# Attention and MoE in one kernel: a new order for norms, turns and sums in the first attention

## The chip, the cores and the metric

The kernel runs on one core of a Trainium2 chip. The metric is the device time of one execution in microseconds; the median of several runs is taken. Engines: PE (matmul), ACT (ScalarE), DVE (VectorE), POOL (GpSimd), SP (DMA queues).

## What is computed

Attention with normed q and k over 8 batches, 12 heads, 448 positions, head width 64, and then a two-layer network with a gelu between (768 to 2048 to 768) on all 3,584 tokens:

```
q_n, k_n = rmsnorm(q, g_q), rmsnorm(k, g_k)          # over the 64 of a head
attn = softmax(q_n @ k_n.T / 8)                      # (8, 12, 448, 448)
x = (attn @ v) -> (3584, 768)                        # heads side by side
out = gelu_tanh(x @ w_in) @ w_out                    # 768 -> 2048 -> 768
```

## The kernel before

The work goes batch by batch. Within a batch the 12 heads are taken in NCH = 3 groups `c` of four heads, and the 448 positions as 7 blocks `t` of 64. A *unit* is one pair (c, t): four small matmuls (64 by 64 weights, 448 columns) that make scores, keys on the partitions and queries along the columns, in one of two PSUM score tiles that alternate. In the first attention unit number i is (i // 7, i % 7), so i runs from 0 to 20. Units 2 to 13 get a constant added by four more matmuls ahead of the scores (L342). ACT turns a unit's scores into exponentials (`exp`, L355), in a buffer `ex` for all seven blocks of a group; there are two such buffers, so that group 2 (units 14 to 20) writes the one that group 0 had.

`products(b, c, what, lo, hi)` multiplies the exponentials of blocks lo to hi - 1 on PE (L400): with `what` 0 by ones, which gives the sums of the softmax (here *sums*), with 1 by v (here *V products*). Each block is a *group* of four small matmuls, two into each of two PSUM tiles. The sums are turned by DVE (`turned`, L411), inverted (`recip`, L416), spread again (`spread`, L423), and multiplied with the V products into `xT` (`quad_x`, L441), the input of the first layer. `mm1_pair` and `mm1` (L565, L450) are the first layer: PE matmuls of 128 by 128 weights over pieces of `xT`; pieces 2c and 2c + 1 come of group c.

Ahead of a unit's scores, q and k have to be squared (`square`), summed over the head (`total`, L174, DVE), taken to the power -1/2 (`rsqrt`, ACT: a logarithm L199, then exponentials L215, L218 into PSUM for DVE and L206 into SBUF for GpSimd), multiplied (`normed`, L277, on DVE or POOL), turned by PE (`turn`, L295) into a PSUM tile, and copied to SBUF by DVE (`put`, L304 for k, L308 for q). `t_first` is blocks 0 to 3 and `t_rest` blocks 4 to 6, so that k can go in two pieces. The roots for DVE stand in PSUM: those of group 1 in spare columns of the second of the two tiles `oall` that the products of the first attention write (`place`), those of the last group in a tile of their own from the pool `ps_m`, which has two buffers and also gives the tiles for the turns and for sums (`spared`).

The order of instructions on every engine is written out by hand: `first_attention` emits, for every i, the unit, its exponential, and then the entries of the list `mid` with that number. What an entry does is queued on its engine behind what earlier entries gave it; waits between engines follow from the tiles that are read and written. After unit 20 the function emits the last sums and V products and the first pieces of the first layer. GpSimd's list holds the norms of group 2's q, squares of the next batch, and the issue of the transfers of w_in, w_out and v.

Of the kernel before, what the change touches and what calls it, by code (L numbers as in the profile page):

```python
# [17 lines left out]
def kernel(  # L18
# [11 lines left out]
    nc = tc.nc  # L30
# [147 lines left out]


    oall = [ps_o.tile([128, 512], F32, tag=f"o{r}", name=f"o{r}") for r in range(2)]  # L180
    roots, places = {}, {}

    def place(b, c):
        if (b, c) == (0, NCH - 1):
            t = ps_m.tile([128, 512], F32, tag="mm", name="root")[:, :4 * NT]
        else:
            i = c % 2 * 4 * NT
            t = oall[1][:, S + i:S + i + 4 * NT]
        roots["qk", b, c] = t.rearrange("p (n a t) -> p n a t", n=2, a=2)
        for n in range(2):  # L190
            roots.setdefault(("qk"[n], b, c), roots["qk", b, c][:, n])
        return t

    def rsqrt(b, c=slice(0, NCH), ns=both, near=(), ts=slice(0, NT), twice=False):

        if b not in rinvs:
            rinvs[b] = smp.tile([P, NCH, 2, 2, NT], F32, tag="rinv", name="rinv")
# [12 lines left out]
        if near:  # L210
# [5 lines left out]
            else:  # L216
                t = roots["qk"[near[0]], b, c]
                nc.scalar.activation(t[:, :, ts], lg[:, c, near[0], :, ts], AF.Exp, scale=-0.5)  # L218
        to_sbuf([n for n in range(2)[ns] if n not in near])

    def rsqrt_newton(b):

# [65 lines left out]
    tps = {}  # L288

    def turn(b, c, n, ts=slice(0, NT)):  # L290

# [136 lines left out]
    def recips():  # L428
        recip()
        spread()  # L430
# [144 lines left out]
        )  # L575

    early, late = range(HP - 2), range(HP - 2, HP)
    even, odd = early[::2], early[1::2]

    STEADY = (  # L580
# [135 lines left out]
    def first_attention(side, mid):  # L716

        for i in range(NCH * NT):
            for fn in side.get(i, ()):
                fn()  # L720
            unit(0, i // NT, i % NT)
            exp(0, i // NT, i % NT)
            for fn in mid.get(i, ()):
                fn()
        nc.scalar.preload_act_table_set(GELU_SET)
        c = NCH - 1
        products(0, c, 0, 6)
        turned()
        products(0, c, 1, 5)
        recips()  # L730
        mm1_pair(0, even)
        quad_x(0, c)
        mm1_pair(1, even)
        mm1_pair(0, odd)
        mm1_pair(1, odd)

        mm1(0, 4, early)
        mm1_pair(0, late)
        mm1_pair(1, late)
        square(1, 1, "q", nc.scalar)  # L740
        mm1(0, 4, late)
# [55 lines left out]
    def warm():  # L797
        return oall[0][:, :S]
# [67 lines left out]
    def turn_new(c, ts):  # L866
        tps["k"] = ps_m.tile([128, 1024], BF16, tag="mm", name="tp")
        turn(0, c, "k", ts)

    mid = [(0, lambda: idle(1, warm())),  # L870
           (1, lambda: square(0, 1, "k", nc.scalar, slice(1, 2)),
            lambda: total(0, 1, "k", slice(1, 2)),
# [5 lines left out]
           (4, lambda: idle(1, warm())),  # L878
           (5, lambda: turn(0, 1, "q"), lambda: put(0, 1, "q")),
           (6, lambda: turn_new(1, t_first), lambda: put(0, 1, "k", slice(0, 1)),  # L880
            lambda: put(0, 1, "k", slice(1, 4)),
            lambda: total(0, 2, "q"), lambda: total(0, 2, "k")),
           (7, lambda: products(0, 0, 0, 0, 2)),
           (8, lambda: products(0, 0, 0, 2, 5), lambda: normed(0, 1, "k", nc.vector, t_rest),
            lambda: rsqrt(0, 2, near=(1,)), lambda: normed(0, 2, "q", nc.gpsimd),
            lambda: square(1, 0, "q", nc.gpsimd), lambda: w_in_part(1, 2),
            lambda: square(1, 0, "k", nc.gpsimd),
            lambda: w_out_part(0, 4), lambda: w_out_part(4, 8),
            lambda: square(1, 2, "q", nc.gpsimd), lambda: square(1, 2, "k", nc.gpsimd),
            lambda: w_out_part(8, 12), lambda: w_out_part(12, 14),  # L890
            lambda: w_out_part(14, 16), lambda: load_v(1, 0, 2), lambda: load_v(1, 2, 4),
            lambda: normed(0, 2, "k", nc.vector, t_first)),
# [165 lines left out]
```

## Time and profile before

| | |
|---|---|
| median of 3 runs | 393.44 us (393.36 to 393.51) |
| the profiled execution | 394.93 us |
| its span, first to last instruction | 392.9 us |
| granted PE clock | 0.999 |
| PE, ACT, DVE, POOL busy in the span | 384.7, 277.7, 237.2, 124.3 us |

The profile is of one execution. The span lacks about 2 us around it. In a row of a timeline stand the start, the length, the engine, the line of the kernel, the operation, what it writes and reads with shapes, the number of instructions merged, and in brackets the idle time of the engine before it with what ended it. Starts are counted from the span's start.

### The profile page before, as it was taken

The page shows a single profiled execution, that of the slowest core. Times are in us where ns is not written, and L with a number is a line of the kernel's source. Part 1 is how long each engine was busy: PE and PEld are TensorE (multiplying, and loading weights), DVE is VectorE, ACT ScalarE, POOL GpSimd, SP SyncE. Part 2 cuts the span into 40 slices and gives each one's busy share as a digit, 9 for nine tenths or more (in the row PEclk, how much of TensorE's full clock was granted, in tenths as well). Part 3 has the DMA queues.
Part 4 walks back from the last instruction along what each step waited for, and adds up shares of the span by engine and source line. Part 5 has one row for each costly group of instructions (what it writes and reads, how often), then busy time and mean ns, then how long its engine had stood idle before and what let it go on. Part 6 is the DMA issues. An engine that isn't in the chain of part 4 may idle for free.

```text
span 392.9 us, 17557 instructions
## 1 busy us (share of the span) xinstructions
PE 384.7 (98%) x8066; PEld 291.8 (74%) x8066; DVE 237.2 (60%) x369; ACT 277.7 (71%) x354; POOL 124.3 (32%) x106
## 2 busy tenths in 40 slices
PE   8899999989999999999999999999999999999996
PEld 3455567868868788877888778887888778887664
DVE  5888947975589257953589265963599304880010
ACT  6984589757996589946997579946897449944300
POOL 5995504484102740074301840054400900000000
PEclk9999999999999999999999999999999999999999
DMA  8999998999722995269932896159722621120033
GB/s 280 314 230 211 210 153 274 239 199 245 131 65 63 217 220 102 48 110 247 199 82 55 173 261 116 44 100 208 150 60 75 114 53 41 44 64 4 2 81 81
DMA packets 64414, 54.68 MB, mean 139 GB/s; under 512 B 37588, under 2 KB 59988, under 8 KB 64340
## 3 DMA queue, kind: packets, MB, share of 16 engines
q1 hardware_dynamic: 53904, 41.33, 43.9%
q0 software_dynamic: 10128, 11.80, 18.3%
q8 instruction: 63, 1.03, 1.1%
q10 hardware_dynamic: 308, 0.43, 0.3%
q14 instruction: 11, 0.09, 0.1%
HBM read 45.61 MB, written 11.01 MB: 144 GB/s over the span
## 4 chain that ended last, share of the span: by engine, by line
PE 91%; DVE 3%; ACT 3%; issue 1%; DMA 1%; DVEq 0%
PE t L546 32%; PE t L504 30%; PE t L400 9%; PE t L347 7%; PE t L477 5%; PE t L565 4%; ACT ex L355 2%; PE tp L295 1%; PE o L400 1%; DMA rawq<-in_q_dram 1%; PE h L450 1%; DVE ss L174 0%; DVE kT L304 0%; ACT L1014 0%; PE t L342 0%
## 5 line engine op out<-in xcount | busy, mean ns | idle before, releaser
L504 PE MATMUL t<-wout,g 64*64 64x384 bf16 (+1 forms) x3456 | 150.8, 305 | 0.0
L355 ACT ACTIVATE ex<-t,shift 128x896 bf16<-128x896 f32 x156 | 145.2, 1016 | 3.4 <-PE t L347 1.9
L546 PE MATMUL t<-xT,win 64*64 64x448 bf16 x2688 | 128.9, 349 | 1.1 <-issue 1.1
L504 PEld LDWEIGHTS <-g 64*64 64x64 bf16 x3456 | 112.7, 107 | 20.0 <-PE t L504 0.3
L546 PEld LDWEIGHTS <-win 64*64 64x64 bf16 x2688 | 98.0, 107 | 30.6 <-issue 1.5
L552 ACT ACTIVATE g<-t 128x896 bf16<-128x896 f32 x56 | 50.5, 915 | 59.1 <-PE t L546 59.1
L174 DVE TENSOR_REDUCE ss<-sq 128x14 f32<-128x896 f32 (+3 forms) x45 | 44.5, 997 | 53.8 <-ACT sq L163 50.1
L347 PE MATMUL t<-qT,kT 64*64 64x448 bf16 x672 | 58.3, 350 | 0.7 <-DVE shifts L853 0.3
L368 DVE TENSOR_TENSOR es<-ex 128x1792 bf16<-128x1792 bf16 x20 | 21.2, 1058 | 33.2 <-ACT ex L355 33.2
L277 POOL TENSOR_TENSOR nrmq<-rawq,rinv 128x896 bf16<-128x896 f32 (+1 forms) x21 | 34.8, 1657 | 20.2 <-ACT rinv L206 12.2
L802 POOL COPY mark<-es 1x1 bf16<-1x1 bf16 x6 | 1.1, 178 | 117.7 <-DVE es L375 113.6
L277 POOL TENSOR_TENSOR nrmk<-rawk,rinv 128x896 bf16<-128x896 f32 x20 | 33.6, 1680 | 0.0
L400 PE MATMUL t<-ex,vb 64*64 64x448 bf16 x588 | 31.9, 350 | 0.0
L347 PEld LDWEIGHTS <-kT 64*64 64x64 bf16 x672 | 25.4, 106 | 6.9 <-DVE kT L304 1.5
L411 DVE STREAM_TRANSPOSE st<-t 128x448 f32<-128x448 f32 x42 | 24.7, 627 | 9.1 <-PE t L400 9.1
L400 PEld LDWEIGHTS <-vb 64*64 64x64 bf16 x672 | 23.0, 107 | 7.5 <-issue 0.8
L423 DVE STREAM_TRANSPOSE rb<-rc 128x896 f32<-128x896 f32 (+1 forms) x25 | 26.7, 1067 | 0.3
L710 DVE COPY osb<-t 128x384 f32<-128x384 f32 (+1 forms) x4 | 2.0, 507 | 35.2 <-PE t L477 35.2
L436 DVE TENSOR_TENSOR xT<-t,rb 128x896 bf16<-128x896 f32 x21 | 22.8, 1085 | 0.8
L165 POOL TENSOR_TENSOR sq<-rawq 128x896 f32<-128x896 f32 (+1 forms) x9 | 13.6, 1511 | 29.3 <-DVE ss L174 29.2
L522 ACT COPY osb<-t 128x768 f32<-128x768 f32 (+1 forms) x18 | 12.6, 698 | 14.0 <-PE t L504 14.0
L371 DVE TENSOR_TENSOR es<-es,ex 128x1792 bf16<-128x1792 bf16 x20 | 21.2, 1062 | 0.7 <-ACT ex L355 0.7
(107 smaller groups left out, 327.7 us busy)
## 6 DMA issues: line engine op xcount, KB each, us to landing
rawq<-in_q_dram SPq DMA_DIRECT2D x23, 448.0 KB, 5.1
rawk<-in_k_dram SPq DMA_DIRECT2D x23, 448.0 KB, 5.8
out_dram<-osb SPq DMA_DIRECT2D x42, 192.0 KB, 2.7
vb<-in_v_dram POOLq DMA_DIRECT2D x6, 672.0 KB, 7.5
win<-in_moe_w_in_dram POOLq DMA_DIRECT2D x8, 384.0 KB, 11.6
wout<-in_moe_w_out_dram POOLq DMA_DIRECT2D x3, 768.0 KB, 18.1
out_dram<-osb SPq DMA_DIRECT2D x24, 96.0 KB, 3.4
vb<-in_v_dram POOLq DMA_DIRECT2D x2, 448.0 KB, 15.3
```

The source lines that it names most:

```text
L174: nc.vector.reduce_sum(sss[b][:, seat(b, c), "qk".index(n), hs, ts], squares(b, c, n, hs, ts), axis=AX.X)
L277: eng.tensor_mul(nrms[n, b, c][:, ts].rearrange("p t a d -> p a t d"), raws[n, b, c][:, :, ts], root[:, :, ts].to_broadcast([P, 2, m, D]),)
L347: nc.tensor.matmul(sc[r * R:(r + 1) * R, a, :S], kT[rs, c, t, r], qT[b][rs, c, :, r], start=not begun, stop=True,)
L355: nc.scalar.activation(exs[b, c][:, t], scs.pop((b, c, t))[:, :, :S], AF.Exp, scale=scale, bias=0.0 if in_psum(b, c, t) else shift)
L368: nc.vector.tensor_add(es, ex[:, :2], ex[:, 2:4])
L400: nc.tensor.matmul(o[r][a * D:(a + 1) * D], vb[b % 2][rs, 2 * c + a, i] if what else ones[rs], es[i][rs, a], start=(i == 0), stop=(i == n ...
L411: nc.vector.transpose(oas["st"][:, r].rearrange("p a b -> p (a b)"), o[r])
L423: nc.vector.transpose(oas["rb"][:, rs].rearrange("p r s -> p (r s)"), rc.to_broadcast([128, (rs.stop - rs.start) * m, 32]),)
L436: nc.vector.tensor_mul(xT[b][:, 2 * c:2 * c + 2], oas["o", c, 1][:, :, :S], oas["rb"])
L504: mm = nc.tensor.matmul(o[a * R:(a + 1) * R, bank, :hi - lo], g[rs, f, at:at + R], wout[rs, f, lo:hi], start=(turn == 0 and f == 0), stop= ...
L546: mm = nc.tensor.matmul(h[a * R:(a + 1) * R, j, :S], win[rs, c, at:at + R], xT[b][rs, c], start=begin and c == cs[0], stop=end and c == cs ...
L552: nc.scalar.activation(g[:, 2 * i:2 * i + 2, (b % 2) * S:(b % 2 + 1) * S], h[:, :, :S], AF.Gelu_apprx_tanh,)
```

## The change

- The norm of the middle group's k rest (`normed(0, 1, "k", nc.vector, t_rest)`) goes from entry 8 to entry 6, ahead of the totals of group 2.
- The roots of group 2 are made in entry 9 instead of 8, now both into SBUF too (`also`); POOL norms q of group 2 in two pieces and the rest of its k, which DVE did in entry 12. The transfers and squares behind it on POOL stay behind it; w_in's second part now goes ahead of both squares of group 0 of the next batch.
- q of group 2 is turned into the tile that holds the roots (`tps["last"]`, the same bank), in two pieces (`turn_last`), each followed by its put. Before it had a tile of its own and was turned at once.
- The turn of the middle k's rest goes from entry 10 to 9, the V products of group 0 end behind unit 15 instead of behind unit 14, and the sums and V products of group 1 shift likewise.
- All sums of group 2 stand ahead of its V products; the first two pieces of the first layer's first pair of tiles stand between them.

```diff
     def place(b, c):
         if (b, c) == (0, NCH - 1):
-            t = ps_m.tile([128, 512], F32, tag="mm", name="root")[:, :4 * NT]
+            own = ps_m.tile([128, 512], F32, tag="mm", name="root")
+            tps["last"] = own.bitcast(BF16)
+            t = own[:, S:S + 4 * NT]
...
-        to_sbuf([n for n in range(2)[ns] if n not in near])
+        to_sbuf([n for n in range(2)[ns] if also or n not in near])
...
         products(0, c, 0, 6)
         turned()
-        products(0, c, 1, 5)
         recips()
-        mm1_pair(0, even)
+        mm1_pair(0, early[:2])
+        products(0, c, 1)
         quad_x(0, c)
-        mm1_pair(1, even)
-        mm1_pair(0, odd)
-        mm1_pair(1, odd)
+        mm1_pair(0, early[2:])
+        mm1_pair(1, early)
...
+    def turn_last(ts):
+        tps["q"] = tps["last"]
+        turn(0, 2, "q", ts)
+        put(0, 2, "q", ts)
+
...
            (6, lambda: turn_new(1, t_first), lambda: put(0, 1, "k", slice(0, 1)),
-            lambda: put(0, 1, "k", slice(1, 4)),
+            lambda: put(0, 1, "k", slice(1, 4)), lambda: normed(0, 1, "k", nc.vector, t_rest),
             lambda: total(0, 2, "q"), lambda: total(0, 2, "k")),
            (7, lambda: products(0, 0, 0, 0, 2)),
-           (8, lambda: products(0, 0, 0, 2, 5), lambda: normed(0, 1, "k", nc.vector, t_rest),
-            lambda: rsqrt(0, 2, near=(1,)), lambda: normed(0, 2, "q", nc.gpsimd),
-            lambda: square(1, 0, "q", nc.gpsimd), lambda: w_in_part(1, 2),
-            lambda: square(1, 0, "k", nc.gpsimd),
+           (8, lambda: products(0, 0, 0, 2, 5)),
+           (9, lambda: products(0, 0, 0, 5), lambda: turn(0, 1, "k", t_rest),
+            lambda: put(0, 1, "k", t_rest), lambda: turned(rs=range(1)),
+            lambda: rsqrt(0, 2, near=(1,), also=True),
+            lambda: normed(0, 2, "q", nc.gpsimd, t_first),
+            lambda: normed(0, 2, "q", nc.gpsimd, t_rest),
+            lambda: normed(0, 2, "k", nc.gpsimd, t_rest), lambda: w_in_part(1, 2),
+            lambda: square(1, 0, "q", nc.gpsimd), lambda: square(1, 0, "k", nc.gpsimd),
...
-            lambda: normed(0, 2, "k", nc.vector, t_first)),
-           (9, lambda: products(0, 0, 0, 5)),
-           (10, lambda: turn(0, 1, "k", t_rest), lambda: put(0, 1, "k", t_rest),
-            lambda: turned(rs=range(1))),
-
-           (11, lambda: turn(0, 2, "k", t_first), lambda: put(0, 2, "k", t_first),
-            lambda: turned(rs=range(1, 2))),
-           (12, lambda: turn(0, 2, "q"), lambda: put(0, 2, "q"),
-            lambda: normed(0, 2, "k", nc.vector, t_rest), lambda: recip(),
+            lambda: normed(0, 2, "k", nc.vector, t_first), lambda: turned(rs=range(1, 2))),
+
+           (12, lambda: turn(0, 2, "k", t_first), lambda: put(0, 2, "k", t_first),
+            lambda: turn_last(t_first)),
+           (13, lambda: turn_last(t_rest), lambda: recip(), lambda: products(0, 0, 1, 0, 3),
             lambda: spread(slice(0, 1))),
-           (13, lambda: products(0, 0, 1, 0, 3), lambda: turn_new(2, t_rest),
-            lambda: put(0, 2, "k", t_rest), lambda: spread(slice(1, 2))),
-
-           (14, lambda: products(0, 0, 1, 3), lambda: quad_x(0, 0)),
-           (15, lambda: spared(), lambda: products(0, 1, 0, 0, 4)),
-           (16, lambda: products(0, 1, 0, 4), lambda: turned(), lambda: recips()),
-           (17, lambda: products(0, 1, 1, 0, 4)),
-           (18, lambda: products(0, 1, 1, 4), lambda: quad_x(0, 1)),
-           (19, lambda: spared(), lambda: products(0, 2, 0, 0, 3)),
-           (20, lambda: products(0, 2, 0, 3, 5), lambda: products(0, 2, 1, 0, 5),
-            lambda: products(0, 2, 0, 5, 6))]
+           (14, lambda: turn_new(2, t_rest), lambda: put(0, 2, "k", t_rest),
+            lambda: spread(slice(1, 2)), lambda: products(0, 0, 1, 3, 5)),
+           (15, lambda: products(0, 0, 1, 5), lambda: quad_x(0, 0),
+            lambda: spared(), lambda: products(0, 1, 0, 0, 2)),
+           (16, lambda: products(0, 1, 0, 2, 5)),
+           (17, lambda: products(0, 1, 0, 5), lambda: turned(), lambda: recips()),
+           (18, lambda: products(0, 1, 1, 0, 3)),
+           (19, lambda: products(0, 1, 1, 3), lambda: quad_x(0, 1)),
+           (20, lambda: spared(), lambda: products(0, 2, 0, 0, 6))]
```

More of the change, by code (lines that the diff above doesn't have):

```diff
@@ L180 @@
     oall = [ps_o.tile([128, 512], F32, tag=f"o{r}", name=f"o{r}") for r in range(2)]
-    roots, places = {}, {}
+    roots, places, tps = {}, {}, {}
     def place(b, c):
         if (b, c) == (0, NCH - 1):
-            t = ps_m.tile([128, 512], F32, tag="mm", name="root")[:, :4 * NT]
+            own = ps_m.tile([128, 512], F32, tag="mm", name="root")
+            tps["last"] = own.bitcast(BF16)
+            t = own[:, S:S + 4 * NT]
         else:
@@ L192, in place, with rsqrt @@
         return t
-    def rsqrt(b, c=slice(0, NCH), ns=both, near=(), ts=slice(0, NT), twice=False):
+    def rsqrt(b, c=slice(0, NCH), ns=both, near=(), ts=slice(0, NT), twice=False, also=False):
         if b not in rinvs:
@@ L286, in qT_of @@
         return qT[b]
-    tps = {}
     def turn(b, c, n, ts=slice(0, NT)):
@@ L577 @@
     early, late = range(HP - 2), range(HP - 2, HP)
-    even, odd = early[::2], early[1::2]
     STEADY = (
```

## The prediction

> **What bounds the kernel now.** I read the page first, for what the end is made of, then the busy time of each engine by stretches, and then the timelines of the stretch that is edited, one engine at a time.
>
> ```profile
> PE 384.7 (98%) x8066; PEld 291.8 (74%) x8066; DVE 237.2 (60%) x369; ACT 277.7 (71%) x354; POOL 124.3 (32%) x106
> PE 91%; DVE 3%; ACT 3%; issue 1%; DMA 1%; DVEq 0%
> ```
>
> The first is the busy time of the engines, the second the chain that ended last: PE carries it. The stretches:
>
> ```profile
> 15.90:24.70 8.80, 7.92 (x137) 4.19 (x133) 7.81 (x15) 6.73 (x11) 8.03 (x11) 1.00 1.14 249
> 24.70:31.10 6.40, 5.96 (x110) 3.53 (x106) 5.05 (x9) 6.38 (x7) 6.39 (x6) 1.00 1.12 219
> 31.10:36.40 5.30, 5.30 (x55) 2.85 (x44) 4.09 (x7) 1.30 (x2) 2.94 (x5) 1.00 1.13 210
> 36.40:80.20 43.80, 43.75 (x732) 29.14 (x730) 35.34 (x76) 35.06 (x44) 15.64 (x15) 1.00 1.03 218
> ```
>
> Each row gives the length, then busy time and instruction count of PE, PEld, DVE, ACT and POOL, then the granted clock, DMA share and GB/s. From 31.1 us PE has no idle time worth the name, at the full clock. So the end moves by as much as PE's arrival at its unbroken run moves, and only the first attention, up to there, can move it. Inside it no engine is the bound alone: from 15.9 to 24.7 PE is busy 7.92 of 8.80 us, DVE 7.81; from 24.7 to 31.1 ACT is busy 6.38 of 6.40. The order of waits decides. All edits lie in those two stretches, and the work of PE in them is the same before and after. The profiled span is 392.9 us; that execution lasted 394.93, against a median of 393.44, so what I work out is a difference of spans, and I add it to the median.
>
> The rows that carry the argument, from the timelines of PE, and then of ACT, DVE and POOL (one row with a bar is from the groups of that stretch by shape, with count, busy time and mean ns; the last is the page's for the w_in transfers, with size and us to landing):
>
> ```profile
> 15.93 0.55 PE L400 MATMUL o<-ex,ones 64*64 64x448 bf16 x8
> 16.31 0.36 PE L342 MATMUL t<-eighth,shifts 64*64 64x448 bf16 x4
> 16.49 0.36 PE L347 MATMUL t<-qT,kT 64*64 64x448 bf16 x4
> ...
> 17.44 0.36 PE L347 MATMUL t<-qT,kT 64*64 64x448 bf16 x4
> 17.63 0.35 PE L400 MATMUL o<-ex,ones 64*64 64x448 bf16 x2
> 18.48 0.57 PE L400 MATMUL o<-ex,ones 64*64 64x448 bf16 x6 [0.50 <-DVE nrmk L277]
> ...
> 20.21 0.38 PE L347 MATMUL t<-qT,kT 64*64 64x448 bf16 x4 [0.20 <-DVE kT L304]
> 20.53 0.40 PE L295 MATMUL tp<-ident,nrmk 128*128 128x128 bf16 x4
> ...
> 23.23 0.34 PE L295 MATMUL tp<-ident,nrmk 128*128 128x128 bf16 x3
> 23.50 0.38 PE L347 MATMUL t<-qT,kT 64*64 64x448 bf16 x4
> 23.71 0.93 PE L400 MATMUL o<-ex,vb 64*64 64x448 bf16 x16
> 24.47 0.36 PE L347 MATMUL t<-qT,kT 64*64 64x448 bf16 x4
> ...
> 30.76 1.13 PE L400 MATMUL o<-ex,vb 64*64 64x448 bf16 x18 [0.15 <-DVE xT L441]
> 31.55 0.72 PE L400 MATMUL os<-ex,ones 64*64 64x448 bf16 x8
> 31.93 0.72 PE L400 MATMUL o<-ex,vb 64*64 64x448 bf16 x8
> 32.58 3.20 PE L565 MATMUL t<-xT,win 128*128 128x448 bf16 x16
> 35.62 0.92 PE L450 MATMUL h<-xT,win 128*128 128x448 bf16 x4
> 36.38 0.92 PE L565 MATMUL t<-xT,win 128*128 128x448 bf16 x4
> ```
>
> ```profile
> 16.15 1.73 ACT L355 ACTIVATE ex<-t 128x896 bf16<-128x896 f32 x2 [0.17 <-PE t L347]
> 18.00 0.23 ACT L199 ACTIVATE lg<-ss 128x28 f32<-128x28 f32 x1
> ...
> 18.48 1.90 ACT L355 ACTIVATE ex<-t 128x896 bf16<-128x896 f32 x2
> 20.65 1.75 ACT L355 ACTIVATE ex<-t 128x896 bf16<-128x896 f32 x2 [0.26 <-PE t L347]
> 22.61 0.92 ACT L355 ACTIVATE ex<-t 128x896 bf16<-128x896 f32 x1 [0.21 <-PE t L347]
> 24.72 6.39 ACT L355 ACTIVATE ex<-t,shift 128x896 bf16<-128x896 f32 x7 [1.20 <-PE o L400]
> 15.37 0.61 DVE L304 TENSOR_SCALAR kT<-tp,gcols 128x128 bf16<-128x128 bf16 x2 [0.21 <-PE tp L295]
> 15.90 1.08 DVE L174 TENSOR_REDUCE ss<-g 128x14 f32<-128x896 f32 x1
> 17.89 0.55 DVE L277 TENSOR_TENSOR nrmk<-rawk,o 128x384 bf16<-128x384 f32 x1
> 20.96 0.48 DVE L304 TENSOR_SCALAR kT<-tp,gcols 128x512 bf16<-128x512 bf16 x1 [0.25 <-PE tp L295]
> 22.09 0.62 DVE L308 COPY qT<-tp 128x896 bf16<-128x896 bf16 x1
> ...
> L304 DVE TENSOR_SCALAR kT<-tp,gcols 128x384 bf16<-128x384 bf16 x4 | 1.6, 402 | 0.6 <-PE tp L295 0.6
> ...
> 6.42 1.05 POOL L277 TENSOR_TENSOR nrmq<-rawq,rinv 128x512 bf16<-128x512 f32 x1 [0.39 <-POOL gbf L812]
> 21.94 2.52 POOL L788 DMA_DIRECT2D win<-in_moe_w_in_dram  x4
> ...
> win<-in_moe_w_in_dram POOLq DMA_DIRECT2D x8, 384.0 KB, 11.6
> ```
>
> Three things are to be seen. At 17.63 two matmuls of a sum run, into the first of the two output tiles; the third, into the second tile, waits for the norm of the middle k's rest. That norm reads its roots from other columns of that same tile: a read anywhere in the bank holds PE's write. At 24.72 exponential 14 starts 1.20 us late, when the 16 V products of 23.71 have ended (24.64): it writes the buffer that they read, so it waits for the last of them. And at 30.76 PE waits for the scaled outputs (xT), then runs to 36.38 and on. Constants that I use below: a group of four small matmuls takes 0.19 us (16 in 0.76) and delivers 0.36 after its start; exponentials start 0.82 us apart with their result at 0.92 (rows 16.15, 22.61), from number 14 on 0.89 apart (7 in 6.39); a handover between engines takes 0.04 to 0.08 (18.44 to 18.48, 24.64 to 24.72), mostly 0.05; DVE starts an instruction 0.08 before the end of the last (15.90 against 15.37 + 0.61); a change from small to 128-wide PE work, or back, about 0.1 (23.23 to 23.50 for three transposes of 0.06).
>
> **The middle k's rest ahead of the totals.** The norm (0.55) moves from 17.89 to 15.90, right behind the two puts of row 15.37, and the totals go behind it. The wait at 18.48 goes. But the first sums of 15.93 write the bank that it reads, so their second tile now waits until 16.45 + 0.05 = 16.50: 0.57 of PE, with unit 8's scores queued behind it. They end at 16.85 + 0.57 = 17.42, and exponential 8 starts at 17.47 instead of 16.97. Unit 9 follows 0.57 later too (18.01), exponential 9 at 18.41, no longer behind the roots. The roots' three steps (0.48, from 18.00 to 18.48) now lie behind it, since the totals end 0.46 later, so exponential 10 starts at 18.41 + 0.82 + 0.48 = 19.71, against 19.46. The early transposes and put of the k's rest (all before 19.6) do remove the wait at 20.21: exponentials 11 and 12 start at 20.53 and 21.35, the latter 0.13 earlier than before. Net so far: nothing lost.
>
> **GpSimd norms q in two parts and the last k's rest.** The trace has one piece of 512 columns, 1.05 us; for 384 columns I estimate 0.79 (1.05 x 384/512; bounds 0.55, DVE's time, and 1.05). With the roots at 19.70 the three end at about 20.9, 21.7 and 22.5 (22.8 at the bound); PE wants them at 21.2, 22.5 and 23.7. Hidden by 0.3 at the least; without that cover the excess would stand in the chain below. Behind them on POOL's queue the four w_in transfers are issued at 22.5 instead of 21.94, then squares, w_out and v up to 1.7 later. A w_in transfer takes 11.6 us to land while DMA moves 210 to 249 GB/s in every stretch, so it mostly stands in line behind others; issued 0.5 later it stands in line for less. I cost this at nothing; if that line is empty, at 0.5. DVE loses the last norm (0.55) and puts q in two pieces (0.48 + 0.40 for the 0.62 of 22.09).
>
> **The last q turned in the roots' tile, in two parts.** Units alternate between two score tiles, so unit 12 waits for exponential 10 (19.71 + 0.92 = 20.63); its scores run at 20.89, then eight transposes from 21.18. The k put takes 21.60 to 22.08, the first q put, behind it, ends at 22.48. The second part of q's transposes writes the bank that this put reads, so PE waits until 22.53, with the first V products and unit 14 in line; the transposes end at 22.87 (0.34 as at 23.23), the second put at 22.87 + 0.05 + 0.40 = 23.32, and unit 14 starts at 23.38 (before, 23.50). Between 23.23 and 24.64 lay three transposes, unit 14 and four groups of V products: 1.41. The same now starts at 23.38 with unit 14 ahead of the transposes (one more change of width, 0.1) and unit 15 (0.19) before the last two groups: 1.70, so the V products end at 25.08. That is 0.44 later, and exponential 14 waits for them: 25.16. From there ACT sets the pace for all seven: the last ends at 25.16 + 6.39 = 31.55, against 31.11.
>
> **The last sum ahead of the V products.** Before, PE starts its unbroken run at 30.76, on xT. Now the last group of the sum stands first in line, and waits for exponential 20: PE restarts at 31.60. The DVE chain behind this sum gets more cover (27 groups and wide matmuls between it and the pieces that need it, instead of 22), which frees nothing, since it was not waited for at 36.38. The work left to that point was 5.62 us; now it is 8 groups in place of 8.75 (-0.14), the same 20 wide matmuls (0.19 each, 3.04 for 16 from 32.58 to 35.62) and two more changes of width, since four wide matmuls go ahead of the V products (+0.2): 5.68. Arrival at 37.28 instead of 36.38: +0.90.
>
> The step out of small tiles is 0.1 by the rows (the group at 32.30 would end its slot at 32.49, the wide one starts at 32.58). The Trainium skill, in TensorEngine Tiling (Array Packing), Key Properties, says that a change of tiling mode drains TensorE, and TensorE: Matmul & The Clock Gate, Single matmul latency, puts the constant part of a single matmul, which back-to-back ones hide, at about 0.166 us; by that, as an estimate, the two changes cost 0.33 and the sum would be 1.03 (394.5). The rows decide, and speak for the smaller figure.
>
> **Sum.** +0.44 from the V products' end, +0.46 from the wait that takes the place of that on xT and from the extra changes: 0.9 us, so 393.44 + 0.9 = 394.3. Of the two costs before it, 0.57 and 0.50 saved, nothing is counted twice: they are inside exponential 10's start. The bounds of this case: if half the slip at the V products is absorbed, 394.1; with 1.05 for every GpSimd piece, the skill's drain and another few handovers, 394.9.
>
> **Rivals.** First, the slip at the V products is hidden (the q puts are quicker, or PE does not hold for the first): exponential 14 starts where it did, and only the restart on exponential 20 stays: 31.11 + 0.05 + 5.68 = 36.84, so +0.46, 393.9. For it: 0.44 is the sum of two small steps. Against it: both waits are of the kind seen at 18.48. Second, the other side: the change removes the waits that it aims at, 0.50 (18.48), 0.20 (20.21) and 0.15 (30.76), and puts none in their place: -0.85, 392.6. The place is the norm at 15.90; it decides if its read lets the first sums pass, so that everything behind them runs up to 0.57 earlier and the V products end no later than 24.64. Against it stand the rows 18.48 and 24.72. Third, slower still: a stall as in the next row comes twice.
>
> ```profile
> 80.15 1.11 issue
> ```
>
> It is a row of the chain, PE idle with no releaser. With one more in the shifted instruction order, 394.3 + 1.1 = 395.4.
>
> **How the numbers follow.** Forecast 0.58, first rival 0.18, second 0.15, third 0.09. A measurement of this kernel can tell 0.2%, or 0.79 us, from no change; slower begins at 394.23, close to my forecast, which its open costs (more handovers, GpSimd) push up rather than down. I give four fifths of the forecast's chance to slower. Slower: 0.46 + 0.09 = 0.55, and with the upper end of the first rival 0.58; same: 0.12 + 0.15 = 0.27; faster: 0.15. The range from 393.6 to 395.1 leaves out the second rival and half of the third.
>
> **What would show it.** In the profile after: a wait of about 0.55 at the first sums near 16 us for a DVE norm; no wait of the later sums; exponential 14 starting near 25.2 with a wait of about 1.9; a wait of PE of 0.3 for a q put near 22.5; PE restarting near 31.6 on an exponential, and the second wide pieces (L565 behind L450) near 37.3. I'm wrong if exponential 14 starts at or before 24.7, or if PE's run after 31 us is broken by something other than that exponential.

## The result, and the profile after

| | before | after |
|---|---|---|
| median of 10 runs each | 393.60 us (393.28 to 394.49) | 394.54 us (394.12 to 395.09) |
| the profiled execution, and its span | 394.93, 392.9 us | 394.35, 392.5 us |

The ratio is 1.0021, with a 95% interval from 1.0011 to 1.0030: slower by 0.83 us (0.43 to 1.18). These times alone don't settle it: two sets of runs of the kernel before, further down, differ by as much. What shows it are the events in the profiles. The page of after gives the busy time of the engines and the chain that ended last:

```profile
PE 383.1 (98%) x8066; PEld 289.8 (74%) x8066; DVE 237.8 (61%) x369; ACT 277.6 (71%) x354; POOL 125.0 (32%) x108
PE 90%; ACT 5%; DVE 2%; issue 1%; DMA 1%; DVEq 0%
```

The profiled spans go the other way, 0.5 us down (392.93 to 392.46), and have to be taken apart before they say anything. The profile of before holds the stall of 1.11 us (PE idle, no releaser), and no such stall is in the profile of after. And the inputs land at different times in each execution: exponential 7, the first one behind the part that waits for inputs, starts at 16.15 before and 16.30 after. So I measure from there. In before, the second wide pieces (L565 behind L450) begin 20.23 us after exponential 7, in after 21.07: **+0.84 us**. From there to the end of the span it takes 355.45 (less the stall) and 355.09. The stretches of after follow. Their first two cuts lie 0.15 later than those shown of before, as exponential 7 does; the third is again the end of exponential 20, the fourth the second wide pieces, and the last the same time, 80.20 (length, then busy time of PE, PEld, DVE, ACT, POOL, granted clock, DMA share, GB/s):

```profile
16.05:24.85 8.80, 7.69 (x133) 4.14 (x130) 7.27 (x15) 6.61 (x11) 6.20 (x10) 1.00 1.14 254
24.85:31.65 6.80, 5.73 (x108) 3.46 (x101) 4.89 (x9) 6.39 (x7) 6.78 (x7) 1.00 1.12 211
31.65:37.35 5.70, 5.64 (x52) 2.73 (x52) 5.37 (x9) 1.29 (x2) 5.32 (x7) 1.00 1.13 211
37.35:80.20 42.85, 42.85 (x721) 28.87 (x723) 33.56 (x75) 34.14 (x43) 14.12 (x13) 1.00 0.98 215
```

The second stretch grew from 6.40 to 6.80 and the third from 5.30 to 5.70, at the full clock throughout. The first has the same length by the cut, but PE is busy for 7.69 of it instead of 7.92: it waits longer there, and exponential 14 now starts inside the second stretch. PE's timeline of after:

```profile
16.08 0.35 PE L400 MATMUL o<-ex,ones 64*64 64x448 bf16 x2
16.65 0.56 PE L400 MATMUL o<-ex,ones 64*64 64x448 bf16 x6 [0.22 <-DVE nrmk L279]
...
22.63 0.33 PE L295 MATMUL root<-ident,nrmq 128*128 128x128 bf16 x3 [0.18 <-DVE qT L308]
22.89 0.76 PE L400 MATMUL o<-ex,vb 64*64 64x448 bf16 x12
23.48 0.36 PE L347 MATMUL t<-qT,kT 64*64 64x448 bf16 x4
23.77 0.34 PE L295 MATMUL tp<-ident,nrmk 128*128 128x128 bf16 x3
24.04 0.57 PE L400 MATMUL o<-ex,vb 64*64 64x448 bf16 x8
24.45 0.36 PE L347 MATMUL t<-qT,kT 64*64 64x448 bf16 x4
24.64 0.55 PE L400 MATMUL o<-ex,vb 64*64 64x448 bf16 x8
...
31.71 0.38 PE L400 MATMUL os<-ex,ones 64*64 64x448 bf16 x4 [0.23 <-ACT ex L355]
32.02 0.93 PE L565 MATMUL t<-xT,win 128*128 128x448 bf16 x4
32.88 1.52 PE L400 MATMUL o<-ex,vb 64*64 64x448 bf16 x28
34.33 2.44 PE L565 MATMUL t<-xT,win 128*128 128x448 bf16 x12
36.62 0.92 PE L450 MATMUL h<-xT,win 128*128 128x448 bf16 x4
37.37 0.92 PE L565 MATMUL t<-xT,win 128*128 128x448 bf16 x4
```

And ACT, DVE and POOL of after:

```profile
16.30 0.92 ACT L355 ACTIVATE ex<-t 128x896 bf16<-128x896 f32 x1 [0.17 <-PE t L347]
17.63 1.86 ACT L355 ACTIVATE ex<-t 128x896 bf16<-128x896 f32 x2 [0.41 <-PE t L347]
19.87 3.55 ACT L355 ACTIVATE ex<-t 128x896 bf16<-128x896 f32 x4
25.26 6.39 ACT L355 ACTIVATE ex<-t,shift 128x896 bf16<-128x896 f32 x7 [1.84 <-PE o L400]
...
16.05 0.54 DVE L279 TENSOR_TENSOR nrmk<-rawk,o 128x384 bf16<-128x384 f32 x1
22.16 0.41 DVE L308 COPY qT<-root 128x512 bf16<-128x512 bf16 x1
30.81 1.15 DVE L441 TENSOR_TENSOR xT<-o,rb 128x448 bf16<-128x448 f32 x2
...
20.05 1.83 POOL L279 TENSOR_TENSOR nrmq<-rawq,rinv 128x512 bf16<-128x512 f32 x2 [2.60 <-ACT rinv L208]
21.85 0.82 POOL L279 TENSOR_TENSOR nrmk<-rawk,rinv 128x384 bf16<-128x384 f32 x1
```

To be seen are the two new holds of PE, both on a tile that DVE still reads (16.65 for the norm, 0.57 behind the two matmuls ahead of it; 22.63 for the first q put), then exponential 14 at 25.26 with a wait of 1.84, and PE's restart at 31.71 on the last exponential and no longer on xT.

### The profile page after: what moved, and what is told of

Same layout as the page of the kernel before. It is cut to its first block, busy times and chain, and to the rows that moved or that the text cites. A ratio compares the mean times of both kernels' runs of the same rounds, so it can differ in the third digit from the quotient of the medians.

```text
span 392.5 us, 17559 instructions
## 1 busy us (share of the span) xinstructions
PE 383.1 (98%) x8066; PEld 289.8 (74%) x8066; DVE 237.8 (61%) x369; ACT 277.6 (71%) x354; POOL 125.0 (32%) x108
## 3 DMA queue, kind: packets, MB, share of 16 engines
q8 instruction: 63, 1.03, 1.1%
## 4 chain that ended last, share of the span: by engine, by line
PE 90%; ACT 5%; DVE 2%; issue 1%; DMA 1%; DVEq 0%
PE t L546 32%; PE t L504 30%; PE t L400 9%; PE t L347 7%; PE t L477 5%; PE t L565 4%; ACT ex L355 4%; PE o L400 1%; DMA rawq<-in_q_dram 1%; PE tp L295 1%; PE h L450 1%; DVE ss L174 1%; PE t L342 0%; DVE kT L304 0%; ACT L1015 0%
## 5 line engine op out<-in xcount | busy, mean ns | idle before, releaser
L546 PEld LDWEIGHTS <-win 64*64 64x64 bf16 x2688 | 96.6, 107 | 30.6
L279 POOL TENSOR_TENSOR nrmq<-rawq,rinv 128x896 bf16<-128x896 f32 (+2 forms) x22 | 35.0, 1590 | 22.4 <-ACT rinv L208 12.0
L279 POOL TENSOR_TENSOR nrmk<-rawk,rinv 128x896 bf16<-128x896 f32 (+1 forms) x21 | 34.4, 1639 | 0.0
```

The costliest lines, as they stand in the source:

```text
L279: eng.tensor_mul(nrms[n, b, c][:, ts].rearrange("p t a d -> p a t d"), raws[n, b, c][:, :, ts], root[:, :, ts].to_broadcast([P, 2, m, D]),)
L546: mm = nc.tensor.matmul(h[a * R:(a + 1) * R, j, :S], win[rs, c, at:at + R], xT[b][rs, c], start=begin and c == cs[0], stop=end and c == cs ...
```

## The experiments

All are measured by the same events, counted from the start of exponential 7 of each profile. "Rest" is from the second wide pieces to the end of the span. The first four expectations count from the start of the first exponential. From there to exponential 7 it is 7.12 in before and in after, but 7.25 in sums later, 7.93 in q at once and 7.35 in last part alone, as the inputs landed, so I count from exponential 7. Times and ratios are against runs of the kernel before on the same chip; its medians there were 394.17 for sums later to last part undone, 394.13 for both waits undone, norm moved alone, V products whole and laid out, and 394.34 for the other four.

| kernel | exp. 7 at | exp. 14 | second wide pieces | rest | median | ratio (95%) |
|---|---|---|---|---|---|---|
| before | 16.15 | 8.57 | 20.23 | 356.56 | 393.60 | |
| after | 16.30 | 8.96 | 21.07 | 355.09 | 394.54 | 1.0021 (1.0011 to 1.0030) |
| sums later | 16.01 | 8.53 | 20.65 | 355.27 | 394.03 | 0.9998 (0.9985 to 1.0012) |
| q at once | 16.94 | 8.67 | 20.79 | 354.86 | 394.27 | 1.0003 (0.9990 to 1.0016) |
| last part alone | 17.16 | 8.57 | 20.68 | 355.13 | 394.66 | 1.0014 (1.0003 to 1.0024) |
| last part undone | 16.32 | 8.96 | 21.33 | 355.73 | 395.35 | 1.0032 (1.0020 to 1.0044) |
| both waits undone | 16.16 | 8.07 | 20.18 | 354.93 | 393.80 | 0.9995 (0.9983 to 1.0007) |
| norm moved alone | 16.34 | 8.45 | 20.11 | 355.18 | 394.30 | 1.0002 (0.9988 to 1.0015) |
| V products whole | 16.03 | 8.77 | 20.88 | 355.56 | 394.24 | 1.0006 (0.9991 to 1.0022) |
| k's rest on DVE | 15.99 | 9.06 | 21.18 | 354.83 | 393.97 | 1.0002 (0.9986 to 1.0018) |
| laid out | 16.52 | 6.95 | 20.36 | 354.92 | 393.42 | 0.9981 (0.9960 to 1.0002) |
| laid out, repeat 1 | 16.19 | 6.95 | 19.25 | 354.87 | 392.79 | 0.9953 (0.9936 to 0.9971) |
| laid out, repeat 2 | 17.36 | 6.95 | 20.79 | 356.22 | 394.20 | 0.9997 (0.9975 to 1.0019) |
| before, repeat | 16.04 | 8.57 | 20.23 | 355.18 | 393.57 | 0.9975 (0.9961 to 0.9988) |

A span is the sum of its three parts: 16.30 + 21.07 + 355.09 = 392.46 for after. The first part depends on when inputs land. The third lies between 354.8 and 355.7 in all but two profiles, and those two have the stall of 1.0 to 1.1. Where this scatter of 0.9 comes from stays open; it is as large as the effect, so a single span can't show how much of a later arrival reaches the end. The second part is steady: exponential 14 is at 8.57 in all three profiles that have before's front, and at 6.95 in all three of the laid-out one. So this measure tells 0.1 us, where the medians tell perhaps 1.

**Sums later.** The changed kernel, with group 0's first sums one unit later, so that the norm that held them has ended:

```diff
-           (7, lambda: products(0, 0, 0, 0, 2)),
-           (8, lambda: products(0, 0, 0, 2, 5)),
-           (9, lambda: products(0, 0, 0, 5), ...
+           (8, lambda: products(0, 0, 0, 0, 3)),
+           (9, lambda: products(0, 0, 0, 3), ...
```

> The kernel after, with the first five sums of group 0 one unit later (three behind unit 8, four behind unit 9), so that the norm of the middle k's rest has ended when the first sum writes the bank that it reads. I measure the stretch from the start of the first exponential to PE's arrival at the last pieces of the first layer (27.35 us in the profile before, 28.19 after). Forecast's theory (the new wait at the first sums runs through exponentials 8 and 10 to the V products' end and so to exponential 14): exponential 14 starts 0.5 us earlier against the first than after, stretch 27.7, time 0.5 under the kernel after. Rival (the wait is hidden as the old one at 18.48 was; the loss lies in the q turn and the last sum alone): stretch 28.2, no change of time.

Measured: 20.65, 0.42 less than in after. From the first exponential (8.76) to the second wide pieces (36.66) it is 27.90, 0.29 less than in after, between the theory's 27.7 and the rival's 28.2; the inputs took 0.13 of the gain. Exponential 14 is 0.43 earlier, where 0.5 was expected. ACT's timeline of this kernel:

```profile
16.01 2.54 ACT L355 ACTIVATE ex<-t 128x896 bf16<-128x896 f32 x3 [0.17 <-PE t L347]
```

Three exponentials run without a gap: number 8 follows 7 at once (0.81 instead of 1.33). The wait at the first sums is in the path.

**q at once.** The changed kernel, with both parts of q's turn ahead of one put, so that no transposes wait for a put:

```diff
-    def turn_last(ts):
+    def turn_last():
...
-        turn(0, 2, "q", ts)
-        put(0, 2, "q", ts)
+        turn(0, 2, "q", t_first)
+        turn(0, 2, "q", t_rest)
+        put(0, 2, "q")
```

> The kernel after, with the last q turned into the roots' tile all at once behind unit 12 and put in one copy, so that PE waits for no put between two parts. Forecast's theory (the put of the first part and the turn of the second stand in the chain to unit 14 and the V products): stretch 27.75, 0.45 less than after; time 0.4 to 0.5 under the kernel after. Rival (the loss comes from the first sums' wait; the q turn is covered by ACT): stretch 28.1 to 28.2, time as after.

Measured: 20.79, 0.28 less than in after, where 0.45 was expected. (From the first exponential it is 28.71, with exponential 7 itself 0.81 later.) The wait for the q put is in the path too. The missing 0.17 is another wait: turned at once, the second part of q comes to PE before GpSimd has normed it, as the timeline of PE's weight loads shows:

```profile
22.59 0.17 PEld L295 LDWEIGHTS <-nrmq 128*128 128x128 bf16 x3 [0.17 <-POOL nrmq L279]
```

**The last part alone.** The kernel before, with the new order behind unit 20 (all sums of group 2 ahead of its V products, four wide matmuls between):

```diff
-        products(0, c, 1, 5)
         recips()
-        mm1_pair(0, even)
+        mm1_pair(0, early[:2])
+        products(0, c, 1)
...
-           (20, lambda: products(0, 2, 0, 3, 5), lambda: products(0, 2, 1, 0, 5),
-            lambda: products(0, 2, 0, 5, 6))]
+           (20, lambda: products(0, 2, 0, 3, 6))]
```

> The kernel before, with only the last part of the change: all sums of group 2 ahead of its V products, and the order of the first pieces of the first layer with it. Forecast's theory (PE then restarts on exponential 20 instead of on xT, and changes width twice more): exponential 14 as before, stretch 27.75, which is 0.4 more than before; time 0.4 over the kernel before. Rival (the sums first let the DVE chain start earlier, which pays): stretch 27.35 or less. Rival that gives the whole loss to this part: stretch 28.2, time 0.85 over the kernel before.

Measured: 20.68, 0.45 more than before (28.03 from the first exponential), with exponential 14 where it was (8.57). PE's timeline of this kernel has the wait that was forecast:

```profile
32.17 0.38 PE L400 MATMUL os<-ex,ones 64*64 64x448 bf16 x4 [0.52 <-ACT ex L355]
32.49 0.93 PE L565 MATMUL t<-xT,win 128*128 128x448 bf16 x4
```

**The last part undone.** The changed kernel with the order behind unit 20 as it was before (the same diff turned round).

> The kernel after, with the last part put back as before: V products of group 2 between its sums. If the two costs of the forecast simply add, stretch 27.75, 0.45 under after. But laid out from the rows after, xT of group 1 now ends at 31.96, later than exponential 20's end at 31.66, and the V products wait for it: then the old order costs more, not less: stretch 28.5, 0.3 over the kernel after. So this tells whether the last sum ahead of the V products is a cost in itself or only in the kernel before.

Measured: 21.33, 0.26 more than after (28.45 from the first exponential, where 28.5 was expected). PE's timeline of this kernel:

```profile
31.50 0.38 PE L400 MATMUL o<-ex,vb 64*64 64x448 bf16 x2 [0.19 <-DVE xT L441]
32.03 1.13 PE L400 MATMUL o<-ex,vb 64*64 64x448 bf16 x18 [0.16 <-DVE xT L441]
```

PE waits twice for xT of group 1. In before these outputs end 0.64 after exponential 20 starts (14.56 against 13.92), in after 1.34 (15.66 against 14.32), so V products that overwrite what they read cannot start. The new last part avoids that wait. It costs 0.45 on the old front and saves 0.26 on the new one.

**Both waits undone.** The first two edits together.

> The changed kernel with its two front waits taken out: the first sums go one unit later (no block of them ahead of the middle k's rest's norm), and q of group 2 is turned at once with one put. All else, the last part too, as in the changed kernel. Alone, the later sums brought 0.42 us and q at once 0.28 of the stretch from the start of exponential 7 to the second wide pieces (21.07 in the changed kernel, 20.23 in the one before). Theory (both waits stand in one chain, which ends at exponential 14): the two gains add up but for a small rest, the V products end some 0.1 earlier again than with the later sums alone, so exponential 14 starts at about 8.0 after exponential 7 (8.96 changed, 8.57 before) and PE is there after 20.1 (19.95 to 20.4): at or just under the time of the kernel before, 393.1 to 394.0 where that has 393.6. Rival A (the gains are of one wait, seen twice): no better than 20.6. Rival B (behind exponential 14 another wait, the roots' exponentials or GpSimd's norms, takes over): exponential 14 at 8.5, 20.6.

Measured: exponential 14 at 8.07 and 20.18. The two gains, 0.42 and 0.28, bring 0.89 together, 0.19 more than their sum. Most of this is the wait of 0.17 for GpSimd in q at once, which is gone here. With the first sums later, the roots come earlier, and GpSimd starts 3.09 after exponential 7 (3.76 in q at once), while q's turn comes only 0.43 earlier (4.83 and 5.26). ACT's timeline of this kernel:

```profile
16.16 2.53 ACT L355 ACTIVATE ex<-t 128x896 bf16<-128x896 f32 x3 [0.17 <-PE t L347]
24.23 6.40 ACT L355 ACTIVATE ex<-t,shift 128x896 bf16<-128x896 f32 x7 [1.21 <-PE o L400]
```

Exponential 14 is 0.50 earlier than before, and the second wide pieces only 0.05: the last part takes back 0.45.

**Norm moved alone.** The kernel before with the middle k's rest's norm ahead of the totals, nothing else:

```diff
-            lambda: put(0, 1, "k", slice(1, 4)),
+            lambda: put(0, 1, "k", slice(1, 4)), lambda: normed(0, 1, "k", nc.vector, t_rest),
...
-           (8, lambda: products(0, 0, 0, 2, 5), lambda: normed(0, 1, "k", nc.vector, t_rest),
+           (8, lambda: products(0, 0, 0, 2, 5),
```

> The kernel before with one move alone: the norm of the middle k's rest goes ahead of the totals of group 2, so the wait of 0.50 at the sums of 18.48 goes, and one of about 0.55 at the first sums comes. Theory: one wait replaces the other, exponential 8 starts 0.5 later (1.3 after exponential 7 instead of 0.81), but q's one put and the V products are met as before, so the stretch to the second wide pieces is 20.2 (20.1 to 20.4) as in the kernel before, no change in time. Rival A (the removed wait is worth its length): 19.7. Rival B (the new wait is not made up, since the totals and roots are 0.5 later too): 20.7 and 0.5 us slower.

Measured: 20.11, 0.12 less than before, where no change to 0.2 more was expected. The wait moved and became shorter, as PE's timeline of this kernel shows: it is 0.58 from two matmuls of a sum to the next (0.85 in before, from 17.63 to 18.48):

```profile
16.12 0.35 PE L400 MATMUL o<-ex,ones 64*64 64x448 bf16 x2
16.70 0.57 PE L400 MATMUL o<-ex,ones 64*64 64x448 bf16 x6 [0.22 <-DVE nrmk L277]
```

Exponential 8 is 0.53 later, but exponential 11 already 0.10 earlier (4.40 against 4.50). So in before's order the wait at the first sums costs no more than the wait that it replaces. That doesn't make it free: sums later took it out of the changed kernel, put nothing in its place, and gained 0.42. What before's order would gain with neither wait was not tried.

**V products whole.** The changed kernel, with the last two blocks of group 0's V products ahead of unit 15's scores:

```diff
-            lambda: spread(slice(1, 2)), lambda: products(0, 0, 1, 3, 5)),
-           (15, lambda: products(0, 0, 1, 5), lambda: quad_x(0, 0),
+            lambda: spread(slice(1, 2)), lambda: products(0, 0, 1, 3)),
+           (15, lambda: quad_x(0, 0),
```

> The changed kernel with one edit: the last two blocks of group 0's V products go ahead of unit 15's scores instead of behind them. Theory (exponential 14 waits for the last of these products, with unit 15's four matmuls of 0.19 in front): exponential 14 starts 0.2 earlier, 8.77 after exponential 7, and the second wide pieces at 20.88 (20.8 to 20.95); in time 0.2 us less, which the times alone cannot tell. Rival (PE is held by the put of q, so that the order behind it does not matter, or unit 15's scores are then too late for their exponential): 21.07, no change.

Measured: 8.77 and 20.88, as the theory has it. The four matmuls of unit 15 (0.19) stand in front of the products that exponential 14 waits for.

**k's rest on DVE.** The changed kernel, with the norm of the last group's k's rest back on DVE:

```diff
-            lambda: normed(0, 2, "k", nc.gpsimd, t_rest), lambda: w_in_part(1, 2),
+            lambda: w_in_part(1, 2),
...
-           (13, lambda: turn_last(t_rest), lambda: recip(), ...
+           (13, lambda: turn_last(t_rest), lambda: normed(0, 2, "k", nc.vector, t_rest), lambda: recip(), ...
```

> The changed kernel with the norm of the last group's k's rest given back to DVE, between q's second put and the reciprocal; GpSimd norms only q. Theory (GpSimd's norm of it, 0.82, is hidden, and on DVE the 0.54 stands in front of the reciprocal and the spreads, which the scaled outputs of group 0 and with them the tiles for the sums of group 1 wait for): exponential 14 as in the changed kernel, 8.96, the second wide pieces 21.07 to 21.3 (laid out from the rows: 21.24), 0 to 0.2 us slower. Rival (GpSimd's norm is late and holds PE): stretch 20.7 or less, faster.

Measured: exponential 14 at 9.06, where 8.96 was expected, and the second wide pieces at 21.18, in their range and 0.11 more than after. The loss comes ahead of exponential 14. The transposes of the k's rest wait for DVE's norm, and start 7.57 after exponential 7 instead of 7.47, by the timeline of PE's weight loads of this kernel:

```profile
23.56 0.17 PEld L295 LDWEIGHTS <-nrmk 128*128 128x128 bf16 x3 [0.35 <-DVE nrmk L279]
```

GpSimd's 0.82 for this norm is hidden in after, and its use here is worth 0.1.

**Laid out.** If the waits of the front are what it costs, an order without them should be faster than both. So I laid the first attention out anew from the durations in the rows: no sum between a score and the norm that it waits for, and group 0's V products done ahead of exponential 14. Its core:

```diff
-           (7, lambda: products(0, 0, 0, 0, 2)),
-           (8, lambda: products(0, 0, 0, 2, 5)),
+           (6, lambda: products(0, 0, 0, 0, 1), ..., lambda: products(0, 0, 0, 1, 2)),
+           (7, lambda: products(0, 0, 0, 2, 3), ..., lambda: products(0, 0, 0, 3, 4)),
+           (8, lambda: products(0, 0, 0, 4, 5), ..., lambda: products(0, 0, 0, 5, 6)),
...
+           (12, lambda: products(0, 0, 1, 0, 1), ..., lambda: products(0, 0, 1, 2, 3), ...
+           (13, lambda: products(0, 0, 1, 3, 6)),
+           (14, lambda: products(0, 0, 1, 6, 7), ...
...
+           (20, lambda: products(0, 2, 0, 4, 5), lambda: mm1_pair(0, early[:2]), ...
```

> The first attention in another order, laid out by hand from the rows: sums of group 0 one unit earlier and one block at a time, so that none of them stands between a score and the norm that it waits for; the V products of group 0 end ahead of the point at which exponential 14 needs their buffer; k's rest on DVE; q of group 2 turned in the roots' tile in two parts, but with the V products' first blocks and not a unit's scores behind its put; the sums and V products of groups 1 and 2 closer behind their exponentials. Theory (the first attention's order alone sets when PE begins its unbroken run, and that sets the time): exponential 14 follows exponential 13 without a wait to speak of, at about 7.0 after exponential 7 (8.57 before, 8.96 changed), the second wide pieces begin at about 18.2 (20.23 and 21.07), and the kernel takes some 2 us less than the one before, 391.3 to 392.2 where that has 393.6. Rival (what is gained there is waited for later, at the transfers of w_in and w_out that land at 38 and 53 us, or at the norms of the next batch): the stretch is shorter by 2 us and the time by less than 0.8, with a wait of PE of over 1 us between 36 and 60 us.

Measured: exponential 14 at 6.95 as expected, but the second wide pieces at 20.36 instead of 18.2. PE's timeline of this kernel says where the rest went:

```profile
29.02 0.35 PE L565 MATMUL t<-xT,win 128*128 128x448 bf16 x1
31.35 0.73 PE L565 MATMUL t<-xT,win 128*128 128x448 bf16 x3 [1.99 <-DMA win<-in_moe_w_in_dram]
```

The first wide pieces ask for w_in before it is there. The rival had the right kind of cause and the wrong place: the wait is for the first part of w_in at 29 us, not for anything between 36 and 60.

**Loads later, three kernels.** To get w_in's first part earlier I put the loads of the next batch's middle group behind it: at unit 12 instead of 7, at unit 18, and the same in the kernel before as a control.

```diff
-            (7, lambda: loads(1, 1))]
+            (12, lambda: loads(1, 1))]
```

> The laid-out first attention with one edit: the loads of the next batch's middle group (q and k) are issued at unit 12 instead of unit 7, so behind the first part of w_in on the transfers' way. In the laid-out kernel PE waited 1.99 us at 29.02 to 31.35 for that first part, which landed at 31.22, and the second wide pieces began 20.36 after exponential 7 instead of the 18.2 expected. Theory (transfers are served in the order of issue at a fixed rate, so the two loads, 1.2 to 1.3 us each in the rows, stood in front of w_in): the first part lands by 28.9, the wait shrinks to 0.3 or less, the stretch is 18.4 (18.2 to 18.7), and the time is 391.3 to 392.3 where the kernel before has 393.6 to 394.1. Rival (the rate itself is the limit, whatever the order): w_in lands at 30.5 or later, the wait stays over 1 us, stretch 19.5 or more, or the wait moves on to the second part of w_in or to w_out, with PE idle over 0.8 us between 36 and 56 us.

> As the last, with those loads at unit 18, behind the second part of w_in too. Theory: the stretch is the same 18.4; the second part of w_in lands 2.5 us earlier than there (about 36 instead of 38.7) and is not waited for; no further change in time. If PE waits for the second part of w_in with the loads at unit 12, this version is faster than that one by that wait. Rival: the loads are now late for the squares of that group on ACT, whose gelus stand behind: PE idle or ACT waiting near 38 us, 0.5 to 1 us slower than with unit 12.

> The kernel before with the same edit alone, the loads of the next batch's middle group at unit 12. Theory (there the first part of w_in lands at 30.32 and PE asks for it at 32.58, so nobody waits): stretch 20.23 as before, no change in time. Rival (the order of transfers is worth something by itself, so the gain of the laid-out kernel with later loads is not the order's in the first attention): 0.5 us or more faster, or slower by the loads' lateness.

The edit did nothing. Up to there SP has only loads in its queue, runs ahead of the units, and issues each as soon as one of the four buffers is free (with the edit unit 12's scores run at 20.84, and the loads are issued at 13.83 and 18.39); the order of instructions on every engine is the same with and without the edit. SP's rows in before, laid out, and laid out with the loads at unit 12 are these, one fence each:

```profile
13.73 0.37 SPq L125 DMA_DIRECT2D rawq<-in_q_dram  x1
18.59 0.37 SPq L125 DMA_DIRECT2D rawk<-in_k_dram  x1
```

```profile
14.15 0.37 SPq L125 DMA_DIRECT2D rawq<-in_q_dram  x1
18.71 0.37 SPq L125 DMA_DIRECT2D rawk<-in_k_dram  x1
```

```profile
13.83 0.37 SPq L125 DMA_DIRECT2D rawq<-in_q_dram  x1
18.39 0.37 SPq L125 DMA_DIRECT2D rawk<-in_k_dram  x1
```

So whether an earlier w_in helps wasn't tried. But the three kernels are repeats, and tell two things. First, the laid-out order is tied to w_in: its first part lands 14.70, 13.59 and 15.12 after exponential 7 in the three profiles, and the second wide pieces begin 5.66, 5.66 and 5.67 after that landing. Less PE's wait for it (1.99, 0.88 and 2.42), all three would stand at 18.37, an estimate, close to the 18.2 expected. PE's wait in the two repeats, by their timelines:

```profile
29.92 0.73 PE L565 MATMUL t<-xT,win 128*128 128x448 bf16 x3 [0.88 <-DMA win<-in_moe_w_in_dram]
```

```profile
32.62 0.73 PE L565 MATMUL t<-xT,win 128*128 128x448 bf16 x3 [2.42 <-DMA win<-in_moe_w_in_dram]
```

(Landings are those that the trace gives for the transfers.) In before the landing (30.32) was 2.26 ahead of the first use (32.58), so an order that asks for it over 2.3 us earlier meets it, unless the landing moves too. The landing moves with the inputs: in these three profiles GpSimd begins to issue this part of w_in at 15.97, 14.86 and 16.80, behind squares of the inputs, and it lands 14.9 to 15.7 later. So the place to try is GpSimd's list and not SP's; that was not tried. Second, the repeat of before against before gives 0.9975 with an interval that excludes 1: two sets of runs of the same instructions, 393.57 and 394.34. A quarter of a per cent can come from nothing here.

The laid-out order has medians of 393.42, 392.79 and 394.20 in its three sets (30 runs together: median 393.42, lowest 391.84), where before has 394.13 and 394.34 in the same sessions. That is probably some 0.7 us faster, but with what the repeat of before shows I don't call it settled. Its first wide pieces behind the small matmuls (32.01 to 33.84 in the first profile) instead of ahead of them could cover up to 1.8 of the 0.9 to 2.4 us, an estimate; that was not tried.

## Why the prediction came out right

The forecast was +0.90, counted in the times of before. What the runs showed, step by step (times of after less 0.15, for its later start):

- **The norm at 15.90 holds the first sums.** Forecast: exponential 8 at 17.47, exponential 10 at 19.71; measured 17.48 and 19.72. The hold itself is shorter than the 0.57 that was written: PE goes on at 16.50 as forecast, but two of the eight matmuls run ahead of it, and the row names 0.22 of idle time. That the new wait costs no more than the old one is shown by the norm moved alone (-0.12).
- **GpSimd's norms are hidden.** The estimate of 0.79 measured 0.82; they end at 22.5 as forecast, and DVE in place of the last one costs 0.11. The cover for q's second part is thin: in q at once, where PE asks for it sooner, it is waited for. The transfers issued behind them, costed at nothing, hold nobody: PE has no wait after 31.71 in this part.
- **The q turn in two parts.** PE held until 22.48 (forecast 22.53; the row names 0.18 of idle time, 0.3 was forecast), unit 14 at 23.33 (23.38), the V products' end at 25.04 (25.08), exponential 14 at 25.11 (25.16). From exponential 7 that is +0.39 where +0.44 was forecast: the five hundredths entered with the first q put, which ended that much sooner than laid out. One term of this step was tried alone: unit 15's 0.19 ahead of the last V products (V products whole, 0.19).
- **The last part.** Restart at 31.56 (31.60), +0.46 forecast; measured 0.45 alone, and 0.84 - 0.39 = 0.45 in the whole. The first change of width took 0.12 (32.02 - 31.71 less 0.19), the second 0.10 (32.88 - 32.02 less four times 0.19). The Trainium skill's constant of a single matmul, 0.166 us, in TensorE: Matmul & The Clock Gate, Single matmul latency, gave +1.03 for the whole as an estimate; the trace shows the smaller figure.
- **The sum.** 37.28 forecast, 37.22 measured for the second wide pieces; +0.84 by the events where +0.90 was forecast, +0.83 by the times.

What the prediction did not see: its two terms are not properties of the two edits. It added 0.44 for the front and 0.46 for the last part, which is right in that order only. The new front alone costs 1.10 (21.33 against 20.23), since it makes xT of group 1 late as well, and the new last part then brings 0.26. That the forecast of the sum holds all the same is no luck: it laid out both edits together, and the events named above came within 0.06 of it. And "about 0.2% is what a measurement can tell" was too confident: the repeat of before differs by 0.25%, and by that a change of 0.21% can't be told from none by times. That the times agree with the events to 0.01 us is luck. The rival of a second stall fell the other way: the profile of after has none, and of 14 profiles only before's and one other have it.

## What to carry to other kernels

In a hand-ordered pipeline, a wait that is removed is worth what the next wait leaves of it: trace the new order instruction by instruction to the point where one engine runs unbroken, and sum only there. Spare columns of a busy PSUM tile are paid for in PE's order: here PE's writes waited for DVE's reads of other columns at 16.65 and 22.63. And when differences of a few tenths of a per cent matter, compare spans between two events inside the kernel, and run the old kernel against itself once.

## What the runs showed of the hardware

- Exponential 7 starts at 15.99 to 17.36 over the profiles, and at 16.52, 16.19 and 17.36 in the three of the laid-out order, whose instructions are the same. The first inputs land at different times: the load of q issued at 2.2 landed at 8.56, 7.36 and 9.40 there. This alone makes a scatter of over 1 us.
- A stall of PE of 1.0 to 1.1 us with no releaser comes now and then near 81 us: in before, and in the second repeat of the laid-out order, whose PE timeline has it:

```profile
82.93 3.40 PE L546 MATMUL t<-xT,win 64*64 64x448 bf16 x66 [1.03 <-issue]
```

  The repeats with the same instructions lack it, so the order alone does not cause it; what does, stays open.
- GpSimd took 0.82 us for the norm of 384 columns (after) that DVE does in 0.54 (k's rest on DVE); GpSimd's roots stand in SBUF, DVE's in PSUM.
